# A feed-forward product in another seven-product form, and one batch's projection chunks moved together

## The chip, the cores and the metric

The kernel runs on one core of one Trainium2 chip. The metric is the device time of one execution, in microseconds; a comparison uses the median of several runs. One more execution was taken by the hardware profiler, and all durations of single instructions come from that one.

## The reference

For each of 8 batches there are a sequence `x` (8 heads x 512 x 64) and a state (8 heads x 32 x 64). Both attend to each other, and the result goes through a feed-forward layer with an exact GELU:

```python
scores = scale * x @ state^T            # softmax over the 32 states
xread  = softmax(scores) @ state        # 512 rows per batch
sread  = softmax(scale * state @ x^T) @ x   # 32 rows per batch
t   = concat([xread, sread], axis=2)    # (8, 8, 544, 64), heads merged to 512 columns
out = gelu(t.reshape(4352, 512) @ w_in) @ w_out   # w_in 512 x 2048, w_out 2048 x 512
```

Input and output are float32; the kernel multiplies in bfloat16 and accumulates in float32.

## The kernel before

**First product.** The 512 read rows of a batch are never formed. As `xread = a @ state`, the kernel multiplies the state by `w_in` first: `P` (256 rows of head and state x 2048) is made in four column chunks of 512 (`p_mm`, then copies to SBUF). A *block* `M(k)` is then 128 of the 2048 hidden columns for all 512 tokens of a batch: two matmuls of `P` with the transposed softmax weights `AT`, and a GELU on ACT, which writes `g` in bfloat16. A batch has 16 blocks; chunk f of `P` serves blocks 4f to 4f+3.

**Second product.** `g` (tokens x 2048) times `w_out` is done plainly for batch 0. For batches 1 to 7 both are cut in quarters: `g_q(b, h, k)` has token half h and hidden half k, `w_q[k][n]` has hidden half k and column half n. Seven products of quarters (`X(b, name)`, 16 matmuls of 128x256 each) stand in for eight. Some products need a sum or a difference of two quarters of `g` (`g_sum`, a DVE step over 128x2048, into one of three buffers of the pool `apool`) and of `w_out` (`w_sums`, once for all batches). The results are combined by ACT copies, DVE adds and, in the loop, two POOL steps per batch: `u` (line 658) and `v` (line 622). Four PSUM banks, tags `o0` to `o3`, hold the products; two products can be added up in one bank.

**Slots.** The loop over b = 2..7 is a *slot* each, with eight units p = 0..7. A unit issues two blocks of batch b, and most units one product X of batch b-1. Unit 1 also has the scores of batch b+1 (16 matmuls, exp on ACT), units 2 and 3 its normalisation (`norm`, three DVE steps), unit 5 the four chunks of the next `P` (`p_all`) and the first X of batch b, unit 7 the second X of batch b. In the last slot (b = 7) the 256 rows of state reads go through their own first product (`SR`, seven products in two halves g) in units 0 to 4, and through the second one (`R`) after that. The tail behind the loop does batch 7's remaining products; its last two are cut in three pieces (`PIECES`), so that the last copy and transfer are small.

**Order.** All is scheduled by hand: each engine runs its instructions in the order in which the program issues them, and waits in place for what it needs. SP holds the queue of output transfers (`x_out`, `rows_out`, `r_out`) and of the DMA transposes of `x` and of the softmax weights. POOL loads `x` and rearranges it (`rearr`, `rearr_ones`); a one-column copy (`hold_for`) keeps a load back until a given block of `g` is there.

Of the kernel before, what the change touches and what calls it, by code (L numbers as in the profile page):

```python
# [17 lines left out]
def kernel(  # L18
# [541 lines left out]
    w_sum = {}  # L560

    def w_add(name, x, y, op):
        if name == "3":
            pair = persist.tile([128, 2, MH, NH], BF16, name="ws_34", tag="mix0")
            w_sum["3"], w_sum["4"] = pair[:, 0], pair[:, 1]
        elif name != "4":
            tag = {"6": "mix1", "1": "mix2", "7": "mix3"}[name]
            w_sum[name] = persist.tile([128, MH, NH], BF16, name=f"ws_{name}", tag=tag)
        nc.vector.tensor_tensor(out=w_sum[name], in0=x, in1=y, op=op)

    def w_sums(i):
        (b11, b12), (b21, b22) = w_q
        w_add(*(
            ("3", b12, b22, ALU.subtract),
            ("4", b21, b11, ALU.subtract),
            ("6", b11, b12, ALU.add),
            ("1", b11, b22, ALU.add),
            ("7", b21, b22, ALU.add),
        )[i])
# [14 lines left out]
    def g_sum(b, name):  # L594
        (h0, k0), (h1, k1), op = G_SUMS[name]
        t = apool.tile([128, MH, 256], BF16, name="gsum", tag="gsum")
        nc.vector.tensor_tensor(out=t, in0=g_q(b, h0, k0), in1=g_q(b, h1, k1), op=op)  # L597
        xs[b, "g" + name] = t
# [20 lines left out]
    def c22(b):  # L619
        xs[b, "v"] = c_tile("v")  # L620
        o = xs[b, "o", 1]
        nc.gpsimd.tensor_tensor(  # L622
            out=xs[b, "v"], in0=xs[b, "q"], in1=o[:, :, :NH], op=ALU.subtract
        )
        if b < B - 2:
            c22_add(b)

    def c22_add(b):
        o = xs[b, "o", 1]
        nc.vector.tensor_tensor(out=o[:, :, NH:], in0=xs[b, 3], in1=xs[b, "v"], op=ALU.add)  # L630
        x_out(b, 1)

    def X(b, name):
        bank = {"3": 0, "4": 1, "5": 0, "2": 1, "1": 2, "6": 3, "7": 2}[name]
        first = name in "3416"
        if first:
            xs[b, bank] = otile([128, 2, NH], "xp", bank)
        ps = xs[b, bank]
        lhs = {"3": (0, 0), "4": (1, 1)}.get(name)
        lhs = xs[b, "g" + name] if lhs is None else g_q(b, *lhs)  # L640
        rhs = {"5": w_q[1][1], "2": w_q[0][0]}.get(name)
        rhs = w_sum[name] if rhs is None else rhs
        x_mm(ps, lhs, rhs, first)
        if name == "3":
            xs[b, "s3"] = c_tile("s3")
            if b > 1:
                nc.scalar.copy(out=xs[b, "s3"], in_=ps)
            for h in range(2):
                xs[b, "o", h] = hpool.tile([128, 2, d_model], FP32, name="oh", tag=f"oh{h}")
        elif name == "4":  # L650
            xs[b, "s34"] = c_tile("s34")
            nc.vector.tensor_tensor(out=xs[b, "s34"], in0=ps, in1=xs[b, "s3"], op=ALU.add)
        elif name == "5":
            o = xs[b, "o", 0][:, :, NH:]
            nc.scalar.copy(out=o, in_=ps)  # L655
            xs[b, "u"] = c_tile("u")
            x_out(b, 0, right)
            nc.gpsimd.tensor_tensor(out=xs[b, "u"], in0=xs[b, "s34"], in1=o, op=ALU.subtract)  # L658
        elif name == "2":
            nc.scalar.copy(out=xs[b, "o", 1][:, :, :NH], in_=ps)  # L660
            c22(b)
        elif name == "1":
            xs[b, "q"] = c_tile("q")
            nc.vector.tensor_tensor(out=xs[b, "q"], in0=ps, in1=xs[b, "s34"], op=ALU.add)
        elif name == "7":
            nc.vector.tensor_tensor(
                out=xs[b, "o", 0][:, :, :NH], in0=ps, in1=xs[b, "u"], op=ALU.add
            )
            x_out(b, 0, left)
# [8 lines left out]
    both = slice(0, 2)  # L678

    def L4():  # L680
        b = B - 1
        ps = xs[b, 1] = otile([128, 2, NH], "xp", 1)
        x_mm(ps, g_q(b, 1, 1), w_sum["4"], True)
        xs[b, "s34"] = c_tile("s34")
        nc.vector.tensor_tensor(out=xs[b, "s34"], in0=ps, in1=xs[b, "s3"], op=ALU.add)
        xs[b, "y"] = c_tile("q")
        nc.vector.tensor_tensor(out=xs[b, "y"], in0=xs[b, 3], in1=xs[b, "s34"], op=ALU.add)

    def L5():
        b = B - 1  # L690
        x_mm(xs[b, 0], xs[b, "g5"], w_q[1][1], False)
        nc.scalar.copy(out=xs[b, "o", 0][:, :, right], in_=xs[b, 0])
        rows_out(0, both, right, nc.sync)

    def L5_u():
        b = B - 1
        xs[b, "u"] = c_tile("u")
        nc.vector.tensor_tensor(
            out=xs[b, "u"], in0=xs[b, "s34"], in1=xs[b, "o", 0][:, :, right], op=ALU.subtract
        )  # L700

    def L2():
        b = B - 1
        x_mm(xs[b, 1], xs[b, "g2"], w_q[0][0], False)
        c21 = xs[b, "o", 1][:, :, left]
        nc.scalar.copy(out=c21, in_=xs[b, 1])
        rows_out(1, both, left, nc.sync)
        xs[b, "v"] = c_tile("v")
        nc.vector.tensor_tensor(out=xs[b, "v"], in0=xs[b, "y"], in1=c21, op=ALU.subtract)

    PIECES = ((0, 0, NH, 2), (1, 0, NH // 2, 0), (1, NH // 2, NH, 1))

    def l_mm(ps, name, j, n0, n1, first):
        for m in range(MH):
            nc.tensor.matmul(  # L715
                ps,
                lhsT=xs[B - 1, "g" + name][:, m, 128 * j:128 * j + 128],
                rhs=w_sum[name][:, m, n0:n1],
                start=(first and m == 0),
                stop=(m == MH - 1),  # L720
                skip_group_check=True,
            )

    def L1():
        b = B - 1
        for j, n0, n1, at in PIECES:
            ps = xs[b, "x", j, n0] = otile([128, n1 - n0], "xp", at)
            l_mm(ps, "1", j, n0, n1, True)
            nc.vector.tensor_tensor(
                out=xs[b, "o", 1][:, j, NH + n0:NH + n1],  # L730
                in0=ps,
                in1=xs[b, "v"][:, j, n0:n1],
                op=ALU.add,
            )
        rows_out(1, both, right, nc.sync)

    def L7():
        b = B - 1
        for j, n0, n1, at in PIECES:
            ps = xs[b, "x", j, n0]  # L740
            l_mm(ps, "7", j, n0, n1, False)
            nc.vector.tensor_tensor(
                out=xs[b, "o", 0][:, j, n0:n1], in0=ps, in1=xs[b, "u"][:, j, n0:n1], op=ALU.add
            )
            rows_out(0, slice(j, j + 1), slice(n0, n1), nc.scalar if n0 else nc.sync)
# [97 lines left out]
    def r_homes():  # L843
        pair = [att.tile([128, 2, MH, 128], BF16, name="rs", tag="xT") for _ in range(2)]
        one = att.tile([128, MH, 128], BF16, name="rs1", tag="AT")
        homes = [pair[0][:, 0], pair[0][:, 1], pair[1][:, 0], pair[1][:, 1], one]
        rs["homes"] = dict(zip("51267", homes))

    def r_sum(name):
        t = rs["g" + name] = rs["homes"][name]  # L850
        (h0, k0), (h1, k1), op = G_SUMS[name]
        nc.vector.tensor_tensor(out=t, in0=r_q(h0, k0), in1=r_q(h1, k1), op=op)
# [7 lines left out]
    def R(name):  # L860
# [4 lines left out]
        bank = {"3": 0, "4": 1, "5": 0, "2": 1, "1": 2, "6": 3, "7": 2}[name]  # L865
        first = name in "3416"
        if first:
            home = {"3": 1, "4": 2, "6": 2}
            rs[bank] = otile([128, NH], "rp", home[name]) if name in home else ftile([128, NH], "rp")
        ps = rs[bank]  # L870
        lhs = {"3": (0, 0), "4": (1, 1)}.get(name)
        lhs = rs["g" + name] if lhs is None else r_q(*lhs)
        rhs = {"5": w_q[1][1], "2": w_q[0][0]}.get(name)
        rhs = w_sum[name] if rhs is None else rhs
# [9 lines left out]
        add, sub = ALU.add, ALU.subtract  # L884
        if name == "3":
            nc.scalar.copy(out=c_new("s3"), in_=ps)
            for h in range(2):
                rs["o", h] = opool.tile([128, d_model], FP32, name="osb", tag="osb")
        elif name == "4":
            nc.vector.tensor_tensor(out=c_new("s34"), in0=ps, in1=rs["s3"], op=add)  # L890
        elif name == "5":
            o = rs["o", 0][:, NH:]
            nc.scalar.copy(out=o, in_=ps)
            nc.vector.tensor_tensor(out=c_new("u"), in0=rs["s34"], in1=o, op=sub)
        elif name == "1":
# [10 lines left out]
        elif name == "7":  # L906
            nc.vector.tensor_tensor(out=rs["o", 0][:, :NH], in0=ps, in1=rs["u"], op=add)
            r_out(0)
# [379 lines left out]
```

## Time and profile before

| | |
|---|---|
| median of 3 runs | 203.3 us (203.26, 203.30, 203.94) |
| profiled execution | 203.97 us, of which the profile's span is 202.1 us |
| granted TensorE clock | 1.00 |
| PE, matmul | busy 195.0 us (97% of the span) |
| DVE / ACT / POOL | busy 155.9 / 139.2 / 67.3 us |
| one product X | 16 matmuls, 1.75 us on PE |
| two blocks | 4 matmuls, 0.86 us on PE |
| one sum of `g` | mean 1.37 us on DVE, 35 of them |
| slot 3 to slot 4 | unit 0 begins at 72.31 and at 93.52 us |
| slot 4 to slot 5 | unit 0 begins at 93.52 and at 115.33 us |

All times of single instructions are counted from the start of the span. A line of a timeline gives start, duration, engine, line of the program, operation, what is written from what, shapes and a count; in brackets the idle time before it and the instruction that ended it. A line with a count over 1 is a run of instructions whose duration is that of the whole run.

### The profile page before, as it was taken

To read this page: it belongs to the slowest core of one execution; us is meant where nothing else is said; L and a number is where in the kernel's file an instruction comes from. 1 tells how busy PE (TensorE), PEld (TensorE's weight loads), DVE (VectorE), ACT (ScalarE), POOL (GpSimd) and SP (SyncE) were. 2 spreads that over 40 slices of the span, in tenths; PEclk is the share of its full clock that TensorE was granted. 3 is DMA by queue.
4 is the path that set the end of the run, shared out by engine and by line. 5 is a ranking of instruction groups with operands and counts; after the bars stand their busy time and mean duration, and the time that the engine had idled before them with its cause. 6 is when DMAs were issued, how large, how long until landed. Compare 5 with 4: busy or idle time off the path is not lost.

```text
span 202.1 us, 4900 instructions
## 1 busy us (share of the span) xinstructions
PE 195.0 (97%) x2030; PEld 134.4 (66%) x2035; DVE 155.9 (77%) x248; ACT 139.2 (69%) x251; POOL 67.3 (33%) x75
## 2 busy tenths in 40 slices
PE   7899999999999999999999999999999999999992
PEld 2434544465767677667767587677776878878892
DVE  2954875989996799986996967587758888894982
ACT  3785578798986878677967596688859477854020
POOL 8963503424259198431537202410220011200000
PEclk9999999999999999999999999999999999999999
DMA  6999999969665789592875208450107001040135
GB/s 195 196 171 203 205 199 194 181 140 158 89 116 107 208 96 156 116 133 78 107 156 148 63 2 112 146 114 0 52 27 184 3 0 55 0 159 0 52 105 159
DMA packets 40566, 23.16 MB, mean 115 GB/s; under 512 B 21856, under 2 KB 39136, under 8 KB 40544
## 3 DMA queue, kind: packets, MB, share of 16 engines
q0 software_dynamic: 13984, 8.10, 29.4%
q1 hardware_dynamic: 25872, 14.36, 29.3%
q10 hardware_dynamic: 688, 0.39, 0.6%
q8 instruction: 16, 0.26, 0.5%
q14 instruction: 6, 0.05, 0.1%
HBM read 17.30 MB, written 8.91 MB: 130 GB/s over the span
## 4 chain that ended last, share of the span: by engine, by line
PE 91%; DVE 5%; ACT 2%; issue 1%; ACTq 0%
PE xp L603 40%; PE hp L506 26%; PE op L548 5%; PE sp L810 3%; PE rp L876 3%; PE p_ps L441 2%; PE op L532 2%; PE xp L715 2%; PE pt L333 2%; PE warm_ps L150 2%; PE sr L917 1%; ACT P L955 1%; DVE gsum L597 1%; DVE P L955 1%; PE hp L1064 1%
## 5 line engine op out<-in xcount | busy, mean ns | idle before, releaser
L513 ACT ACTIVATE g<-hp 128x512 bf16<-128x512 f32 x124 | 65.9, 607 | 21.1 <-PE hp L506 14.8
L506 PE MATMUL hp<-AT,P 128*128 128x512 bf16 x248 | 61.2, 379 | 0.0
L603 PEld LDWEIGHTS <-gsum 128*128 128x128 bf16 x528 | 51.2, 98 | 11.4 <-DVE gsum L597 0.8
L597 DVE TENSOR_TENSOR gsum<-g 128x2048 bf16<-128x2048 bf16 x35 | 47.3, 1367 | 0.5
L506 PEld LDWEIGHTS <-P 128*128 128x128 bf16 x248 | 23.5, 98 | 20.6 <-issue 0.6
L603 PE MATMUL xp<-ws,gsum 128*128 128x256 bf16 x304 | 36.3, 273 | 0.4 <-DVE gsum L597 0.4
L603 PE MATMUL xp<-ws,g 128*128 128x256 bf16 x224 | 26.7, 272 | 0.3
L603 PE MATMUL xp<-w_out_bf,gsum 128*128 128x256 bf16 x224 | 26.6, 273 | 0.0
L603 PEld LDWEIGHTS <-g 128*128 128x128 bf16 x224 | 21.7, 98 | 5.3 <-issue 1.9
L658 POOL TENSOR_TENSOR u<-s,oh 128x512 f32<-128x512 f32 x6 | 8.8, 1468 | 40.1 <-ACT oh L655 40.1
L225 POOL COPY x<-xb 128x1024 bf16<-128x1024 bf16 x12 | 14.6, 1244 | 17.5 <-DMA xb<-in_x_dram 17.5
L622 POOL TENSOR_TENSOR v<-q,oh 128x512 f32<-128x512 f32 x6 | 8.3, 1379 | 19.5 <-ACT oh L660 17.2
L235 POOL COPY xo<-xb 128x1024 bf16<-128x1024 bf16 x12 | 12.1, 1041 | 5.0 <-PE sr L917 5.0
L955 ACT CAST P<-p_ps 128x512 bf16<-128x512 f32 x25 | 12.7, 606 | 0.1
L356 DVE TENSOR_TENSOR a<-e,ics 128x512 bf16<-128x512 bf16 x14 | 11.7, 834 | 0.5
L548 PE MATMUL op<-w_out_bf,g 128*128 128x512 bf16 x44 | 11.1, 380 | 0.5 <-issue 0.3
L955 DVE CAST P<-p_ps 128x512 bf16<-128x512 f32 x15 | 9.4, 684 | 1.7 <-PE p_ps L441 1.7
L353 DVE TENSOR_REDUCE cs<-e 128x16 f32<-128x512 bf16 x14 | 9.5, 677 | 0.9 <-ACT e L340 0.9
L441 PE MATMUL p_ps<-w_in_bf,sbd 64*32 64x512 bf16 x248 | 9.4, 380 | 0.0
L513 ACT ACT_TABLE_LOAD x7 | 9.0, 1283 | 0.1
L548 PEld LDWEIGHTS <-g 128*128 128x128 bf16 x48 | 4.2, 98 | 5.6 <-issue 0.8
L340 ACT ACT_TABLE_LOAD x6 | 7.7, 1283 | 0.1
(143 smaller groups left out, 240.7 us busy)
## 6 DMA issues: line engine op xcount, KB each, us to landing
out_dram<-oh SPq DMA_DIRECT2D x15, 256.0 KB, 2.5
xb<-in_x_dram POOLq DMA_DIRECT2D x7, 512.0 KB, 5.9
out_dram<-oh SPq DMA_DIRECT2D x6, 512.0 KB, 3.5
w_in_bf<-in_moe_w_in_dram POOLq DMA_DIRECT2D x6, 256.0 KB, 12.2
out_dram<-osb SPq DMA_DIRECT2D x5, 256.0 KB, 3.2
w_out_bf<-in_moe_w_out_dram POOLq DMA_DIRECT2D x4, 256.0 KB, 8.6
w_out_bf<-in_moe_w_out_dram POOLq DMA_DIRECT2D x2, 512.0 KB, 13.5
x0f<-in_x_dram SPq DMA_DIRECT2D x3, 256.0 KB, 3.9
```

Source lines behind the costliest of these rows:

```text
L225: nc.gpsimd.tensor_copy(out=A.x4[:, :, :, 64 * t:64 * t + 64].rearrange("p j c d -> p c j d"), in_=src[:, t],)
L235: eng.tensor_copy(out=A.xo[:, :, :, 2 + 64 * t:66 + 64 * t].rearrange("p j c d -> p c j d"), in_=src[:, t],)
L353: nc.vector.reduce_sum(out=cs, in_=e4, axis=AX.X)
L356: nc.vector.tensor_tensor(out=A.a[:, :, hs].rearrange("p g (c n) -> p g c n", n=NS), in0=e4, in1=ics[:, :, :].to_broadcast((128, G, 2, NS) ...
L441: nc.tensor.matmul(ps[t][32 * c:32 * c + 32, :], lhsT=sbd[64 * t:64 * t + 64, b, c, 32 * t:32 * t + 32], rhs=w_in_bf[64 * t:64 * t + 64, c ...
L506: nc.tensor.matmul(hp, lhsT=Ps[b][:, t, m * 128:(m + 1) * 128], rhs=atts[b].AT[:, :, t, :], start=(t == 0), stop=(t == 1),)
L513: nc.scalar.activation(out=gs[b][:, m, :], in_=hp, func=AF.Gelu)
L548: nc.tensor.matmul(ops[b, j], lhsT=gs[b][:, m, j * 128:(j + 1) * 128], rhs=w_out_bf[:, m, :], start=(m == 0), stop=(m == MC - 1),)
L597: nc.vector.tensor_tensor(out=t, in0=g_q(b, h0, k0), in1=g_q(b, h1, k1), op=op)
L603: nc.tensor.matmul(ps[:, j - js[0], :], lhsT=lhs[:, m, 128 * j:128 * j + 128], rhs=rhs[:, m, :], start=(first and j == js[0] and m == 0), ...
L658: nc.gpsimd.tensor_tensor(out=xs[b, "u"], in0=xs[b, "s34"], in1=o, op=ALU.subtract)
L955: copy(out=Ps[b][:, t, f * 512:(f + 1) * 512], in_=ps[t])
```

## The change

The product becomes another form of seven products. Which quarter stands in which place is fixed by `chain` and `w_diff`; in `chain`, a11 = `q(0,1)`, a12 = `q(0,0)`, a21 = `q(1,1)`, a22 = `q(1,0)`. Three products (1, 2, 4) take a quarter of `g` as it is. The other four take sums that build on one another: 5 = a21 + a22, 6 = 5 - a11, 7 = a11 - a21, 3 = a12 - 6; likewise four of `w_out`. Products 1, 6 and 7 are added up in one bank and read between: after 1 by a DVE add, after 6 by an ACT copy (`u`), after 7 by two DVE adds; 5 and 3 share another bank. Each of 2, 4, 6 and 5 is copied to SBUF by ACT (`snap`); POOL takes no part. Per batch there are four sums of `g` where there were five, four DVE adds as before, four ACT copies where there were three. In a slot the products stand in the order 1, 6, 5, 7 in units 0 to 3, then 3, 2 in unit 5 and 4 in unit 7, where there were 4, 5, 1, 2, then 7, 3 and 6. The matmuls are the same in number and shape.

In slot 2, chunks 2 and 3 of batch 2's `P` were made in units 0 and 3, each behind the unit's blocks. Now both stand in one run behind unit 2's product, and unit 2 issues blocks 4 to 7 while unit 3 issues none.

In the tail, product 5 and the last one, 3, are cut in pieces; product 7 stands whole before 3, with its two adds and one output transfer of 512 KB, where two transfers of 256 KB went out earlier.

```diff
+    def w_diff(name):
...
+        x, y = {
+            "5": (b12, b11),
+            "6": (b22, w_t.get("5")),
+            "7": (b22, b12),
+            "4": (b21, w_t.get("6")),
+        }[name]
+        nc.vector.tensor_tensor(out=w_t[name], in0=x, in1=y, op=ALU.subtract)
...
+    def chain(name, q, got):
+        a11, a12, a21, a22 = q(0, 1), q(0, 0), q(1, 1), q(1, 0)
+        return {
+            "1": (a11,),
+            "2": (a12,),
+            "4": (a22,),
+            "5": (a21, a22, ALU.add),
+            "6": (got.get("5"), a11, ALU.subtract),
+            "7": (a11, a21, ALU.subtract),
+            "3": (a12, got.get("6"), ALU.subtract),
+        }[name]
...
+    BANK = {"2": 0, "1": 1, "6": 1, "7": 1, "5": 2, "3": 2, "4": 3}
...
     def X(b, name):
...
+        x_mm(ps, x_lhs(b, name), w_rhs(name), first)
+        if name == "2":
             if b > 1:
+                snap(b, "c2", "c2", ps)
+        elif name == "4":
+            snap(b, "c4", "c4", ps)
+        elif name == "1":
             for h in range(2):
                 xs[b, "o", h] = hpool.tile([128, 2, d_model], FP32, name="oh", tag=f"oh{h}")
+            add(xs[b, "o", 0][:, :, left], ps, xs[b, "c2"])
+            x_out(b, 0, left)
+        elif name == "6":
+            snap(b, "u", "u", ps)
         elif name == "5":
+            snap(b, "s5", "s5", ps)
+        elif name == "7":
+            add(xs[b, "o", 1][:, :, right], ps, xs[b, "s5"])
+            add(xs[b, "o", 1][:, :, left], ps, xs[b, "c4"])
+            x_out(b, 1)
+        elif name == "3":
+            add(xs[b, "o", 0][:, :, right], ps, xs[b, "u"])
             x_out(b, 0, right)
...
-            M(k, k + 1)
-            if b == 2 and p == 0:
-                pmat(2, 2)
-            if b == 2 and p == 3:
-                p_copy_s(2, 3, p_mm(2, 3, ftile))
+            if b != 2 or p != 3:
+                M(k, k + 1)
+            if b == 2 and p == 2:
+                M(k + 2, k + 3)
             if b == 2 and p == 1:
-                w_sums(4)
-            if p < 4 or (p == 4 and nb == B):
+                w_diff("7")
+            if p < 5 and nb < B:
                 if p == 0:
-                    g_sum(b - 1, "5")
-                    if b > 2:
-                        sr_w("5216"[b - 3])
-                X(b - 1, "45127"[p])
-                if p < 3:
-                    g_sum(b - 1, "127"[p])
+                    g_sum(b - 1, "56")
+                if p == 2:
+                    g_sum(b - 1, "7")
+                if p == 3:
+                    g_sum(b - 1, "3")
+                if p < 4:
+                    X(b - 1, "1657"[p])
+                if b == 2 and p == 2:
+                    for x in [(2, f, p_mm(2, f, ftile)) for f in (2, 3)]:
+                        p_copy(*x)
+                if p == 1 and b > 2:
+                    sr_w("5216"[b - 3])
...
     b = B - 1
-    for name in "521":
-        g_sum(b, name)
-    L4()
-    g_sum(b, "7")
+    g_sum(b, "56")
+    X(b, "1")
+    g_sum(b, "73")
     L5()
-    L5_u()
-    L2()
-    R("7")
-    L1()
-    L7()
+    X(b, "6")
+    R("3")
+    X(b, "7")
+    L3()
```

The state reads' second product `R` takes the same form; its sums are `r_sum("56")` in unit 4 and `r_sum("73")` in unit 5 of the last slot, its products 2, 4 stand in unit 5, 1, 6, 5 in unit 6, 7 in unit 7 and 3 in the tail. The first product of the state reads (`SR`) keeps its form; in unit 0 of the last slot `sr_w("7")` moves from before to behind the products.

## The prediction

> **What bounds the kernel now.** I read the page's shares first, then the chain that ended last, then each engine's timeline around the eight units of a slot. The page's first part and the head of the chain:
>
> ```profile
> PE 195.0 (97%) x2030; PEld 134.4 (66%) x2035; DVE 155.9 (77%) x248; ACT 139.2 (69%) x251; POOL 67.3 (33%) x75
> ...
> PE 91%; DVE 5%; ACT 2%; issue 1%; ACTq 0%
> ```
>
> PE is the bound. In PE's timeline it stands still after 13.2 us only in pieces of tenths; the rest of DVE's 5% lies in the first 13 us, which the change leaves alone. The piece that this change can touch is in slot 4 (PE's timeline; in brackets the wait and its releaser):
>
> ```profile
> 112.93 0.22 PE L424 MATMUL srT<-ident,srm 128*128 128x128 bf16 x1
> 113.57 1.92 PE L603 MATMUL xp<-ws,gsum 128*128 128x256 bf16 x16 [0.42 <-DVE gsum L597]
> ```
>
> From srT to the next product 0.64 us pass here; in slot 3 it is 0.05 (91.72 to 91.77). The stall is worth 0.59.
>
> After X's last matmul, the end is DVE's last piece, its transfer (198.88 + 2.3 to landing = 201.2) and 0.9 us more. So the time is PE's own work plus waits on PE, plus that end. What decides is whether DVE's order feeds PE in time. DVE and POOL in slot 3 and the slot's first product on PE:
>
> ```profile
> 71.62 3.16 DVE L597 TENSOR_TENSOR gsum<-g 128x2048 bf16<-128x2048 bf16 x1
> ...
> 71.67 2.03 POOL L235 COPY xo<-xb 128x1024 bf16<-128x1024 bf16 x2
> ...
> 73.71 1.12 POOL L967 COPY hold<-g 128x1 bf16<-128x1 bf16 x1
> ...
> 75.91 0.68 DVE L652 TENSOR_TENSOR s<-xp,s 128x512 f32<-128x512 f32 x1
> ...
> 76.65 1.96 POOL L225 COPY x<-xb 128x1024 bf16<-128x1024 bf16 x1 [1.01 <-DMA xb<-in_x_dram]
> ```
>
> A sum of 1.22 us takes 3.16 while POOL copies: they do not run together, and POOL, 0.05 later, went first.
>
> **Part by part.** PE's matmuls are the same in number, shape and place, so PE's own work is unchanged but for one item. Durations: a product of 16 matmuls 1.75, a pair of blocks 0.86, a sum 1.22, a DVE add from PSUM 0.69 (a next one starts 0.61 later), norm 1.61 to the next start.
>
> *Removed, hidden already.* One of five g sums per batch (7 x 1.22 on DVE), one of five weight sums (1.25), twelve POOL steps u and v (17.1 us). None is on the chain except the sum at the end of a slot: X6 in unit 7 needed g6, X4 in its place reads g itself. That removes slot 4's stall: **-0.59**.
>
> *P chunks together.* One chunk alone costs PE 0.34 + 0.10 on the next group (51.17 to 51.51, then 1.85 in place of 1.75), two alone 0.88; a run of two at 36.92 costs 0.56 + 0.11 = 0.67. **-0.21**. Blocks 4 to 7 need four PSUM tiles, whose gelus follow on ACT behind the exps (54.4), a table load (1.28), two gelus (1.08) and the u copy (0.59), four at 0.5: they end at about 57.8 to 59.3. The run starts at 59.3: just covered, up to 0.2 if not.
>
> *ACT.* Four copies a batch for three (0.59 more). The c4 copy falls into the 1.4 us idle ahead of the gelus at 137.22, the s5 copy into 0.9 ahead of 145.47: nothing. Without that cover each would be 0.6 a slot.
>
> *New wait in every slot.* X1, X6 and X7 share one bank, so X6 waits until DVE's add has read X1. In slot 6: X1 ends at 139.15, the add runs 139.35 to 140.04, X6 is due at 140.48: 0.44 spare, as scores and a pair of blocks lie between. The chained sums 5 and 6 end by 138.34 there: nothing. SP issues as many transfers as before; the softmax transpose behind `x_out(1)` goes out by 149.3 here (150.85 now) and at 65.5 in slot 2, as now: nothing.
>
> *Slot 3.* Sum 5 ends at 74.78 as now; sum 6 waits for it (74.81 to 76.03); the add starts at 75.95 and ends at 76.64; X6 is due at 76.25 and starts near 76.69: 0.44, or 0.63 if the hold copy (0.19) slips between. Behind it on DVE are two sr_w sums (1.28), norm and sum 7: if POOL's two copies from 76.65 take their 2.0 us first, sum 7 ends at 82.7, when X7 is due at 81.9: 0.8 more. Between 0 (both sums clear POOL) and 1.4 I take **+0.50**, nearest to the row. As to the chain's link: a dependent DVE step starts 0.03 after the end of its source (62.16 after 62.12), an independent one 0.08 before it, so a link costs 0.11. The Trainium skill (VectorE: DVE Perf Modes, The DRAIN you can't avoid) has it that a wait between two such steps costs nothing extra; by that the 0.50 would be 0.39.
>
> *Slot 2.* The order from 50.15: pair, X1, scores (0.47), pair, X6, four blocks, X5 (57.57), the P run (59.32), X7 (59.99), four blocks, X3 at 63.47. DVE's two P copies now stand ahead of norm and sum 3. The first starts 0.51 after the run (51.61 after 51.10), so 59.76; the second 0.60 later; norm 60.96; sum 3 from 62.57 to 63.79; X3 starts at 63.83: **+0.36**. Before, the g sum there had 2 us to spare. The other end: the hold copy at 51.56 meets sum 6, which starts at 51.49. If the sum goes first, hold, the load of x and both POOL copies behind it come 1.1 later, and norm meets them at 62: 1.45. I take the small end, since in slot 3 a sum that was 0.05 ahead lost.
> The Trainium skill (SBUF — State Buffer, Who interferes with whom) says that of such a pair whichever starts first holds the port for its whole instruction. By that rule hold would lose here and the term would be 1.45; the slot 3 row speaks against it at so small a lead.
>
> *Slot 7.* The two adds behind X7 now stand on DVE ahead of the add that reads SR1's bank, into which SR7 accumulates:
>
> ```profile
> 172.96 0.69 DVE L827 TENSOR_TENSOR srt<-srt 128x512 f32<-128x512 f32 x1
> ...
> 174.08 1.49 DVE L831 TENSOR_TENSOR srt<-sp,srt 128x512 f32<-128x512 f32 x2 [0.44 <-PE sp L810]
> ...
> 175.19 0.61 PE L810 MATMUL sp<-srx,srw 128*128 128x128 bf16 x8
> ```
>
> Adds at 173.65 and 174.26, SR1's at 174.87 to 175.56 where it ended at 174.77; SR7 was due at 175.19: **+0.41** (0 to 0.5). The gelus behind it reach R2 with 0.5 spare.
>
> *The end.* X7 starts at 194.82 (its wait for ACT's u copy, 194.78, just fits), its two adds end at 198.07 and only then one transfer of 512 KB leaves, where 256 KB left at 197.11; L3's three pieces follow in the same queue. The last DVE piece stays near 198.9, and the transfers are the end now:
>
> ```profile
> out_dram<-oh SPq DMA_DIRECT2D x15, 256.0 KB, 2.5
> ...
> out_dram<-oh SPq DMA_DIRECT2D x6, 512.0 KB, 3.5
> ```
>
> 198.11 + 3.5 = 201.6 against 201.2 now: 0.4. If the 256 KB of pieces queue wholly behind it at 350 GB/s (the window from 199 to 200 us) it is 0.75 more: 1.15. If mid-kernel traffic swells the 3.5, nothing. I take **+0.60**.
>
> Sum: -0.59 - 0.21 + 0.50 + 0.36 + 0.41 + 0.60 = +1.07. The profiled execution took 203.97 (span 202.1 and 1.9 around it), so 205.0 for its like. The runs' median of 203.3 lies 0.67 below it: 204.4.
>
> **Rivals.** *Not slower:* the freed DVE and POOL do feed PE in time. With u and v gone POOL's copies move, and if slot 3's sum 6 ends before 75.5 and slot 2's sum 3 before 63.4, both chain waits (0.86) vanish: 203.5; below 202.3, where faster by over 0.5% begins, it comes only if slot 7 and the end go too and PE's small gaps at 0.16 close. For it: DVE loses 1.22 us a slot; against it: both spots are set by what DVE waits for, not by its load.
> *POOL first:* slot 2 at 1.45 and slot 3 at 1.3: +1.09 + 0.8, 206.3. For it: leads of 0.05 to 0.1 us decide; against: the row of slot 3.
> *The last transfer hidden:* without the end's 0.60, 203.8. For it: at 200 to 201 us the engines move only 22 GB/s; against: 256 KB more leave 1 us later.
> That X6's wait for the add costs in every slot (the edit does not then do its work) is part of the forecast's wide end only: 0.44 spare was read in a slot where DVE is idle 1.07 before it.
>
> **How the numbers follow.** 0.5%, or 1.02 us, is about what a measurement of this kernel can tell from no change. Forecast 0.47 (204.4 +- 0.5, on the edge: 0.30 slower, 0.17 same); not slower 0.24 (0.18 same, 0.06 faster); POOL first 0.21, slower; transfer hidden 0.08, same. So faster 0.06, same 0.43, slower 0.51. All costs at their small ends give 203.3 - 0.80 = 202.5, all at their large ends (1.4, 1.45, 0.5, 1.15) 207.0; leaving out 1 in 10 on each side, 202.8 to 206.0. The likeliest case's own range is 203.9 to 204.9.
>
> **What would show it.** In the profile after: no PE wait ahead of unit 7's product in slot 4; a PE wait on DVE's add of some 0.4 to 0.6 at X6 in slot 3; one of 0.4 on sum 3 at X3 in slot 2; one of 0.4 at SR7 in the last slot; and 2.2 us or more from the last matmul's end to the last landing, with a 512 KB transfer issued near the last DVE step. It is wrong if X6 waits in slots 4 to 6, if PE waits on ACT, or if the slot length of an undisturbed slot (21.21 us from 72.31 to 93.52) changes.

## The result, and the profile after

The changed kernel takes 206.7 us (median of 6 runs, 206.49 to 207.42), the kernel before 203.62 in the runs beside it: a ratio of 1.0155, interval 1.0127 to 1.0182. It is slower by 3.1 us. The profiled execution took 207.1 us with a span of 205.2, against 203.97 and 202.1, also 3.1 more.

From the page after, the engines' busy times:

```profile
PE 195.5 (95%) x2035; PEld 134.1 (65%) x2035; DVE 142.9 (70%) x234; ACT 142.8 (70%) x260; POOL 50.6 (25%) x63
```

DVE is busy for 13 us less, 11.7 of it in the sums of `g` and `w_out`, and POOL for 17 us less, as the removed combining steps promise. PE's own work is the same within 0.5 us. Yet PE's share falls from 97% to 95%: engines with less to do feed PE later. PE's waits say where. The first is at the start, for a load (line waited in, tile and line waited for; total, times, longest):

```profile
PE xT_ps L271 <- DMA xb<-in_x_dram: 0.7, 1, 0.7
```

The others stand in PE's timeline, whose rows answer to those shown of before:

```profile
65.93 1.92 PE L623 MATMUL xp<-w_out_bf,gsum 128*128 128x256 bf16 x16 [1.73 <-DVE gsum L613]
...
78.93 1.91 PE L623 MATMUL xp<-ws,gsum 128*128 128x256 bf16 x16 [0.25 <-DVE oh L642]
...
115.61 0.22 PE L424 MATMUL srT<-ident,srm 128*128 128x128 bf16 x1
115.67 1.91 PE L623 MATMUL xp<-ws,g 128*128 128x256 bf16 x16
...
177.66 0.61 PE L781 MATMUL sp<-srx,srw 128*128 128x128 bf16 x8 [0.22 <-DVE srt L802]
```

First X3 in slot 2, then X6 in slot 3, then slot 4's end, where the stall is gone (0.06 from srT to the next product, 0.64 before), last SR7. How these add up, from the first product of each slot in the two profiles:

| stretch | before | after | difference |
|---|---|---|---|
| start to the transposes of the second x block (L271) | 19.21 | 19.81 | +0.60 |
| from there to unit 0 of slot 3 | 53.10 | 54.77 | +1.67 |
| slot 3 | 21.21 | 21.62 | +0.41 |
| slot 4 | 21.81 | 21.22 | -0.59 |
| unit 0 of slot 5 to the last matmul's end | 83.19 | 83.56 | +0.37 |
| behind the last matmul | 3.58 | 4.22 | +0.64 |

These give +3.1. The last row is good to 0.05 only, since it rests on spans that are given to 0.1 us. The second row holds the P run (-0.21 by the prediction) and the stall at X3 (so 1.88). Its cause begins 14 us earlier. The timelines of DVE, POOL and SyncE's queue in slot 2, after:

```profile
52.09 1.23 DVE L613 TENSOR_TENSOR gsum<-gsum,g 128x2048 bf16<-128x2048 bf16 x1
...
52.16 1.21 POOL L927 COPY hold<-g 128x1 bf16<-128x1 bf16 x1 [1.41 <-ACT g L513]
...
53.30 0.88 POOL L117 DMA_DIRECT2D xb<-in_x_dram  x1
...
54.35 0.39 SPq L637 DMA_DIRECT2D out_dram<-oh  x1
...
60.35 2.02 POOL L225 COPY x<-xb 128x1024 bf16<-128x1024 bf16 x2 [6.17 <-DMA xb<-in_x_dram]
...
60.51 1.29 DVE L453 CAST P<-p_ps 128x512 bf16<-128x512 f32 x2 [2.31 <-PE p_ps L441]
...
62.31 2.49 POOL L235 COPY xo<-xb 128x1024 bf16<-128x1024 bf16 x2
...
62.71 1.19 DVE L356 TENSOR_TENSOR a<-e,ics 128x512 bf16<-128x512 bf16 x1
...
63.82 2.05 DVE L613 TENSOR_TENSOR gsum<-g,gsum 128x2048 bf16<-128x2048 bf16 x1
```

And POOL and SyncE's queue of before at the same place:

```profile
51.56 0.19 POOL L967 COPY hold<-g 128x1 bf16<-128x1 bf16 x1 [1.41 <-ACT g L513]
...
52.08 0.88 POOL L117 DMA_DIRECT2D xb<-in_x_dram  x1 [0.33 <-POOL hold L967]
...
57.70 0.39 SPq L617 DMA_DIRECT2D out_dram<-oh  x1
...
57.97 2.48 POOL L225 COPY x<-xb 128x1024 bf16<-128x1024 bf16 x2 [5.02 <-DMA xb<-in_x_dram]
```

Sum 6 starts 0.07 us ahead of the hold copy. A copy of one column that took 0.19 now takes 1.21: it ends 0.05 behind the end of the sum. The load that it keeps back goes out at 53.30 in place of 52.08, POOL has its block at 60.35 in place of 57.97, and so POOL's copies run from 60.35 to 64.80, just where DVE has norm's multiplication (1.19 in place of 0.69) and sum 3 (2.05 in place of 1.22). Sum 3 ends at 65.87, X3 starts at 65.93.

Slot 2 itself begins at 50.15 before and at 50.74 after, so 0.6 of each of these differences belongs to the start of the kernel. Counted from the slot's beginning, the load goes out 0.6 later and its block is in use 1.8 later. The other 1.2 is the load itself, 7.05 us from issue to use in place of 5.89. The new form also sends 256 KB of product 1's rows at 54.35, 1.05 behind this load; before, the transfer there left at 57.70, 5.6 behind it. No run moves that transfer alone, so how much of the lateness is the copy's and how much the transfer's is not shown; the P run alone, below, says something on it.

At the end of the kernel, the queue of SyncE after:

```profile
200.62 0.35 SPq L637 DMA_DIRECT2D out_dram<-oh  x1
...
201.09 1.13 SPq L680 DMA_DIRECT2D out_dram<-oh  x2
```

The 512 KB leave at 200.62, 0.36 before the last matmul ends (200.98). The last bytes land at 203.63, 2.65 behind the last matmul; before it was 200.73, 2.2 behind (2.0 and 1.7 behind in the profiles of before once more and of the P run alone, which have the same tail).

### The profile page after: what moved, and what is told of

Same layout as the page of the kernel before. It is cut to its first block, busy times and chain, and to the rows that moved or that the text cites. A ratio compares the mean times of both kernels' runs of the same rounds, so it can differ in the third digit from the quotient of the medians.

```text
span 205.2 us, 4865 instructions
## 1 busy us (share of the span) xinstructions
PE 195.5 (95%) x2035; PEld 134.1 (65%) x2035; DVE 142.9 (70%) x234; ACT 142.8 (70%) x260; POOL 50.6 (25%) x63
## 4 chain that ended last, share of the span: by engine, by line
PE 79%; DMA 8%; POOL 4%; DVE 3%; ACT 2%; issue 1%; DVEq 0%; ACTq 0%; POOLq 0%
PE xp L623 39%; PE hp L506 23%; DMA xb<-in_x_dram 8%; PE op L548 4%; PE rp L847 3%; PE sp L781 3%; POOL w_in_bf L105 2%; PE op L532 2%; DVE oh L642 2%; PE p_ps L441 1%; ACT P L915 1%; PE pt L333 1%; PE sr L877 1%; DVE gsum L613 1%; PE xp L694 1%
## 5 line engine op out<-in xcount | busy, mean ns | idle before, releaser
L623 PEld LDWEIGHTS <-gsum 128*128 128x128 bf16 x416 | 40.4, 98 | 11.7 <-DVE gsum L613 2.2
L623 PEld LDWEIGHTS <-g 128*128 128x128 bf16 x336 | 32.5, 98 | 6.9 <-issue 1.6
L623 PE MATMUL xp<-w_out_bf,g 128*128 128x256 bf16 x224 | 26.7, 273 | 0.3
L613 DVE TENSOR_TENSOR gsum<-g 128x2048 bf16<-128x2048 bf16 x14 | 19.0, 1356 | 0.5
L646 ACT COPY c<-xp 128x512 f32<-128x512 f32 x14 | 8.3, 593 | 9.8 <-PE xp L623 4.5
L623 PE MATMUL xp<-ws,g 128*128 128x256 bf16 x112 | 13.4, 273 | 0.0
L623 PE MATMUL xp<-w_out_bf,gsum 128*128 128x256 bf16 x96 | 11.5, 273 | 1.7 <-DVE gsum L613 1.7
L642 DVE TENSOR_TENSOR oh<-xp,c 128x512 f32<-128x512 f32 x14 | 9.6, 686 | 4.3 <-PE xp L623 4.3
L642 DVE TENSOR_TENSOR oh<-xp,u 128x512 f32<-128x512 f32 (+2 forms) x9 | 5.0, 569 | 9.9 <-PE xp L623 9.9
L613 DVE TENSOR_TENSOR gsum<-g,gsum 128x2048 bf16<-128x2048 bf16 x7 | 9.4, 1339 | 0.0
```

The lines of the kernel that those rows point to most:

```text
L613: nc.vector.tensor_tensor(out=got[name], in0=x, in1=y, op=op)
L623: nc.tensor.matmul(ps[:, j - js[0], :], lhsT=lhs[:, m, 128 * j:128 * j + 128], rhs=rhs[:, m, :], start=(first and j == js[0] and m == 0), ...
L642: nc.vector.tensor_tensor(out=out, in0=x, in1=y, op=ALU.add)
L646: nc.scalar.copy(out=xs[b, name], in_=ps)
```

## The experiments

Below, *body* is the time from the first transpose of L271 to the end of the last matmul: it leaves out the load at the start and the tail, and so shows PE's waits in the slots alone. All but the medians are from profiled executions; the column behind the last matmul is again good to 0.05.

| kernel | body | behind the last matmul | median of runs |
|---|---|---|---|
| before | 179.31 | 3.58 | 203.6 |
| changed | 181.17 | 4.22 | 206.7 |
| hold copy early | 179.85 | 4.18 | 205.31 |
| P copies on ScalarE | 179.28 | 4.24 | 204.64 |
| form alone | 180.32 | 4.17 | 205.63 |
| P run alone | 179.51 | 3.19 | 203.93 |
| adds of X7 late | 180.84 | 4.15 | 206.06 |
| output in halves | 181.22 | 3.81 | 206.16 |
| X5 ahead of X6 in slot 3 | 181.66 | 4.25 | 206.33 |
| four edits | 178.48 | 3.86 | 203.32 |
| four edits, one issue on ScalarE | 178.48 | 3.91 | 203.41 |
| the same, hold copy early | 178.48 | 3.91 | 204.07 |

The runs of before beside these had a median of 203.62 for the changed kernel, 203.81 for the next four, 203.54 for the four after them (adds late to four edits) and 203.42 for the last two.

**The hold copy early.** Theory: the small copy's lost race starts the stall in slot 2.

```diff
-                hold_for(b, 0)
+                hold_for(*((1, 15) if b == 2 else (b, 0)))
```

> In slot 2 the copy that holds back the load of x waits for block 15 of batch 1 instead of block 0 of batch 2, so it runs before sums 5 and 6 start. Theory A (the port): sum 6 took the port 0.07 us ahead of the hold copy, which ended 1.1 us late; the load and POOL's four copies behind it came late and met norm and sum 3. Then PE's wait on sum 3 at X3 falls from 1.73 us to 0.4 or less and the time by 1.3 to 1.9, to about 205.0. Theory B (DVE's order): the two P copies ahead of norm and sum 3 make X3 late whatever POOL does; then the wait stays over 1.2 and the time at 206.7.

Measured 205.31 us, ratio to before 1.0075 (1.0051 to 1.0099). DVE, POOL and PE in slot 2:

```profile
50.07 0.19 POOL L927 COPY hold<-g 128x1 bf16<-128x1 bf16 x1
...
56.95 2.49 POOL L225 COPY x<-xb 128x1024 bf16<-128x1024 bf16 x2 [5.65 <-DMA xb<-in_x_dram]
...
62.68 1.22 DVE L613 TENSOR_TENSOR gsum<-g,gsum 128x2048 bf16<-128x2048 bf16 x1
...
63.96 1.92 PE L623 MATMUL xp<-w_out_bf,gsum 128*128 128x256 bf16 x16 [0.39 <-DVE gsum L613]
```

The copy starts 0.13 ahead of sum 5 (50.20) and takes its 0.19, POOL is out of the way by 61.4, sum 3 takes its 1.22, and X3's wait falls from 1.73 to 0.39. The body is 1.32 shorter. So POOL's late copies made 1.3 of the 1.9 us. The edit does more than remove the race: the load goes out 1.6 us earlier in its slot than it did before the change, and 3.3 ahead of product 1's transfer. The rest is DVE's order: the two P copies ahead of norm and sum 3.

**The P copies on ScalarE.** All four copies of the run on ACT (two of them were on DVE), nothing else.

```diff
-                        p_copy(*x)
+                        p_copy_s(*x)
```

> Both P copies of the run in slot 2 go to ACT, so DVE has none of them ahead of norm and sum 3; the hold stays as it is. Theory B (DVE's order): X3's wait vanishes, the time falls by 1.7 to 1.9, to 204.9. Theory A (the port alone): POOL's late copies still meet norm or sum 3 and hold one of them by 1 to 2 us; X3's wait stays at 0.5 to 1.5. If the wait vanishes here and in the run with the early hold, it takes both: the copies ahead on DVE and POOL's late copies.

Measured 204.64 us, ratio 1.0043 (1.0026 to 1.006). The wait at X3 is gone altogether, though the hold copy is blocked as before:

```profile
51.63 1.21 POOL L927 COPY hold<-g 128x1 bf16<-128x1 bf16 x1 [1.40 <-ACT g L513]
...
59.58 1.22 DVE L613 TENSOR_TENSOR gsum<-g,gsum 128x2048 bf16<-128x2048 bf16 x1 [0.30 <-PE xp L623]
...
59.80 2.89 POOL L225 COPY x<-xb 128x1024 bf16<-128x1024 bf16 x2 [6.14 <-DMA xb<-in_x_dram]
```

Without the P copies, DVE is through with norm and starts sum 3 at 59.58, before POOL's late copies; this time the sum goes first, and POOL waits (2.89). So 0.6 of the 1.9 us is the P copies' alone, and 1.3 need both: the P copies push norm and sum 3 back past 60, and the late load puts POOL's copies there. Each edit alone takes most of it away, which is why the two gains (1.3 and 1.9) don't add. The body is 179.28; the other terms, slots 3 and 7 as measured, put it at 179.31 - 0.59 - 0.21 + 0.41 + 0.38 = 179.30.

**The form alone.** P chunks 2 and 3 back in units 0 and 3, blocks in their units.

```diff
-            if b != 2 or p != 3:
-                M(k, k + 1)
-            if b == 2 and p == 2:
-                M(k + 2, k + 3)
+            M(k, k + 1)
+            if b == 2 and p == 0:
+                pmat(2, 2)
+            if b == 2 and p == 3:
+                p_copy_s(2, 3, p_mm(2, 3, ftile))
...
-                if b == 2 and p == 2:
-                    for x in [(2, f, p_mm(2, f, ftile)) for f in (2, 3)]:
-                        p_copy(*x)
```

> The new form of the product alone; chunks 2 and 3 of batch 2's P stand in units 0 and 3 of slot 2 as in the kernel before, and no block is ahead. My theory: DVE's P copy in unit 0 stands ahead of sums 5 and 6, so sum 6 ends at 54.7 and the add at 55.4 on the clock of before, while X6 is due at 54.5: a PE wait of 0.9 at X6 in slot 2, no wait of 1.7 at X3, and 0.21 for the chunks apart; 0.8 below the changed kernel, 205.9. Rival (the form alone is harmless and the moved chunks do the damage): no wait in slot 2, 205.0 or less.

Measured 205.63 us, ratio 1.0085 (1.0057 to 1.0113). The theory was right in kind: a wait at X6 and none at X3. The timeline of slot 2:

```profile
51.86 0.19 POOL L927 COPY hold<-g 128x1 bf16<-128x1 bf16 x1 [1.40 <-ACT g L513]
...
51.91 0.69 DVE L453 CAST P<-p_ps 128x512 bf16<-128x512 f32 x1 [1.40 <-PE p_ps L441]
...
52.52 1.22 DVE L613 TENSOR_TENSOR gsum<-g 128x2048 bf16<-128x2048 bf16 x1
...
55.65 1.91 PE L623 MATMUL xp<-ws,gsum 128*128 128x256 bf16 x16 [0.65 <-DVE oh L642]
```

Here a P copy still stands ahead of the sums in unit 0, so the first sum starts at 52.52 and the hold copy goes through in 0.19. But the chained sums are then late, and X6 waits 0.65 in slot 2. The change as a whole removed this wait by moving the copy away, and by the same move brought sum 6 onto the hold copy. With the copy in time, POOL has the block at 58.25, 7.8 behind the beginning of the slot, as before.

**The P run alone**, on the kernel before: the block lines of the diff above in the other direction, with the old form kept.

> The kernel before with only the P chunks moved: both in one run behind unit 2's product of slot 2, blocks 4 to 7 ahead. My theory: PE saves 0.21, the two DVE copies stand ahead of norm alone, as this form has no sum in unit 3: 0.2 faster, the same within what can be measured, with slot 2 at 0.2 less. Rival (the moved chunks do the damage by themselves, through the hold copy and POOL): 1 to 2 us slower.

Measured 203.93 us, ratio 1.001 (0.999 to 1.003). Neither the 0.21 nor a loss shows in the runs. In the profile slot 2 takes 22.36 in place of 22.16: a block waits on a P copy of DVE, and what is lost there is more than the 0.21. POOL, and the block's wait on PE:

```profile
52.16 1.08 POOL L967 COPY hold<-g 128x1 bf16<-128x1 bf16 x1 [1.40 <-ACT g L513]
...
53.18 0.88 POOL L117 DMA_DIRECT2D xb<-in_x_dram  x1
...
58.96 2.25 POOL L225 COPY x<-xb 128x1024 bf16<-128x1024 bf16 x2 [4.90 <-DMA xb<-in_x_dram]
...
62.94 1.68 PE L506 MATMUL hp<-AT,P 128*128 128x512 bf16 x7 [0.25 <-DVE P L453]
```

The hold copy loses its race here too, behind a sum of the old form. Yet the block is in use 5.78 behind the load's issue, 0.4 later in its slot than before and not 1.8, and the old form sends its 256 KB only at 57.81. So the lost race by itself did not make the long delay there, and the P copies on DVE and the lost race together, without the new form, cost 0.2. The run brings its gain only where the copies behind it are in time, as in the four edits together below.

**The adds of X7 behind the state adds**, in slot 7: the third argument makes X leave out its adds and its transfer, which `x7_adds` then issues.

```diff
-            X(c, "7")
+            X(c, "7", True)
             SR("1", 1)
             SR("6", 1)
+            x7_adds(c)
```

> In slot 7 product 7's two adds and its output transfer are issued behind the adds of the second half's state products 1 and 6, no longer ahead of them; all else as in the changed kernel. Theory (state product 7 waits because its operand's add stands behind product 7's two adds in VectorE's queue, worth 0.39 us): the 0.22 us wait of the state product on the state add is gone, the time is 0.4 us below the changed kernel's 206.7, some 206.3. Rival (VectorE simply has too much in this stretch, and the two adds come due again at once): a wait of 0.2 to 0.4 us shows up on a later product of slot 7 or on product 3, and the time stays at 206.7.

Measured 206.06 us, ratio 1.0113 (1.008 to 1.0146). No wait is left in slot 7, none came in its place, and the slot is 0.38 shorter (the body 0.33, as slot 2's wait is 1.77 here): the term is as the prediction had it.

**The last 512 KB in two halves.**

```diff
             add(xs[b, "o", 1][:, :, right], ps, xs[b, "s5"])
+            if b == B - 1:
+                x_out(b, 1, right)
             add(xs[b, "o", 1][:, :, left], ps, xs[b, "c4"])
-            x_out(b, 1)
+            x_out(b, 1, left if b == B - 1 else slice(None))
```

> In the last stretch alone, the 512 KB transfer of product 7's rows is sent as two of 256 KB, the right half of the columns after the first add and the left half after the second; all else as in the changed kernel. Theory (the end is later by 0.65 us because 512 KB is issued in one piece behind two adds of about 0.7 us each): the first half starts some 0.7 us earlier and the end comes 0.2 to 0.5 us earlier, 206.2 to 206.5 against 206.7. Rival (the end is set by the small pieces of product 3 and their fixed time from issue to landing, whatever stands ahead of them): the last transfer ends at the same distance from the last matmul as before, 4.2 us, and the time stays at 206.7.

Measured 206.16 us, ratio 1.0124 (1.0088 to 1.016). The body is unchanged (181.22), the tail some 0.4 shorter:

```profile
199.34 0.97 SPq L637 DMA_DIRECT2D out_dram<-oh  x2
```

The first half leaves 0.95 before the last matmul ends (200.29), and from 200.3 to 201.8 the queue moves 83 to 95 KB in each quarter of a microsecond without a break. It looks as if the end waits for the bytes of the last rows; no run changed their number, so that is not shown.

**X5 ahead of X6 in slot 3.**

```diff
-                    X(b - 1, "1657"[p])
+                    X(b - 1, ("1567" if b == 3 else "1657")[p])
```

> In slot 3 alone, product 5 is taken in unit 1 and product 6 in unit 2, so that product 6 no longer stands one unit behind the add that still reads its bank; all else as in the changed kernel. Theory (product 6 loses 0.42 us in slot 3 to the add of product 1, which comes late because sum 6 shares VectorE's port with the hold copy and the block copies): the wait is gone and the time is 0.4 us below 206.7, some 206.3. Rival (slot 3 loses the same time at the next product, because VectorE's queue as a whole is late): a wait of 0.3 us or more on product 6 or 7 in units 2 and 3, and 206.7.

The rival was right. X6's wait is gone, and one on sum 7 comes two units later:

```profile
82.63 1.22 DVE L613 TENSOR_TENSOR gsum<-g 128x2048 bf16<-128x2048 bf16 x1
...
83.91 1.92 PE L623 MATMUL xp<-ws,gsum 128*128 128x256 bf16 x16 [0.59 <-DVE gsum L613]
```

DVE's queue as a whole is late in slot 3. The body is 0.49 longer, 0.36 of it in slot 3. The median, 206.33 (ratio 1.0132, 1.0097 to 1.0167), is all the same not above the changed kernel's. In the profiles the start was 0.72 shorter here (L271 at 19.09); that this holds for the medians too is not shown.

**Four edits together**: the P copies on ScalarE and the three above.

> Four edits on the changed kernel together: the four copies of the P chunks of slot 2 on ScalarE, product 5 ahead of product 6 in slot 3, product 7's adds in slot 7 behind the state adds, and the last 512 KB in two transfers. If the costs found so far are separate and add up: the run with the copies alone gave 204.64; less 0.42, 0.39 and 0.2 to 0.5 this is 203.3 to 203.6, at or a little under the kernel before (203.8 over 20 runs), since the stall of slot 4 that the change removes (0.59) and the P run (0.21) are then not given back. If the waits only move (VectorE is the limit in these stretches): 204.2 to 204.7.

Measured 203.32 us against 203.54 for before, ratio 0.9984 (0.9959 to 1.0009): no difference that these runs can tell. The profile has no wait of PE in slots 2 to 7 that is longer than 0.15, and the body is 178.48, 0.83 under that of before; the prediction's two gains, 0.59 and 0.21, make 0.80. They lie where it put them: slot 4 takes 21.21 in place of 21.81, and slot 2 21.93 in place of 22.16, a length that before has in both its profiles. The swap in slot 3, useless alone, pays once the P copies are off DVE: of the 0.80 between this body and the one with the copies alone, 0.38 is slot 7's term, and the other 0.42 the wait of X6. Of the 0.83 the tail takes back 0.3.

**One issue on ScalarE**, and then the hold copy early on top of it. The second half of the 512 KB goes out through ScalarE's queue; the second kernel adds the first experiment's edit.

```diff
-        x_out(b, 1, left if b == B - 1 else slice(None))
+        if b == B - 1:
+            x_out(b, 1, left, nc.scalar)
+        else:
+            x_out(b, 1)
```

> The four edits together, and in the last stretch the second 256 KB transfer of product 7's rows is issued by ScalarE instead of SyncE. Theory (the end hangs on the last issue of SyncE, which is back to back with four issues and ends 1.08 us after the last matmul with the four edits, 0.5 us before the change): SyncE then has three issues, the last ends some 0.7 us after the last matmul, the span ends 3.5 to 3.6 us after it, not 3.86, and the time is 203.0 against 203.3. Rival (the bytes or the landing time of the last transfers bind): 3.86 us and 203.3.

> As the run before, and in slot 2 the copy that releases the load of block 4 reads the last g tile of batch 1, so that it is free a unit earlier. Theory (with the P copies on ScalarE there is no wait left on sum 3 in slot 2): no difference to the run before, 203.0. Rival (the load of block 4 and the block copies on GpSimd still cost other steps of slots 2 and 3): 0.2 to 0.4 us lower.

The first is 203.41 against 203.42 (ratio 1.0014, 0.9994 to 1.0034); its queues at the end:

```profile
197.14 0.40 ACTq L637 DMA_DIRECT2D out_dram<-oh  x1
197.46 0.85 SPq L690 DMA_DIRECT2D out_dram<-oh  x2
```

SyncE's last issue ends 0.82 behind the last matmul in place of 1.08, and the span still ends 3.91 behind it. The theory that the end hangs on SyncE's issues falls; the last bytes landed 2.2 behind the last matmul in both kernels of this experiment and in the four edits. The second took 204.07 (ratio 1.0022, 1.0007 to 1.0037) with the same body to the hundredth, so the early load is worth nothing once X3 does not wait; its higher median is not in the profile.

**Both kernels once more**, unchanged.

> The kernel before, unchanged, profiled a second time. If the stall of slot 4 (0.42 us on sum 7's operand, of 0.59 that the prediction took off) belongs to every execution, it is there again at product 7 of slot 4; if it comes from one late step of that one execution, it is gone and the span is under 202.1. The lead (first transpose of the second x block at 19.2 us) may move by up to 0.8 us.

> The changed kernel, unchanged, profiled a second time. If the 0.7 us wait on the x load at 19.8 us is no part of the change, the transposes start at 19.0 to 19.3 us and the span is some 204.5; the waits of 1.7 to 1.9 us on sum 3 in slot 2, of 0.25 on the add in slot 3 and of 0.22 in slot 7 are there again.

204.05 and 207.28 us in one run each. The stall of slot 4 is there again in before, to the hundredth:

```profile
113.77 1.92 PE L603 MATMUL xp<-ws,gsum 128*128 128x256 bf16 x16 [0.42 <-DVE gsum L597]
```

In the changed kernel the hold copy again loses to sum 6 by 0.07 (52.11 and 52.18, 1.21 long), and the three waits are 1.91, 0.25 and 0.22. The transposes of L271 start at 19.83 there, which was not expected; they start at 19.01 to 19.51 in the nine kernels that differ from it only in later slots, and at 19.81 in the P run alone. The nine have the same code as it up to there. So the 0.6 at the start is not made by that code. What PE waits for there is loads: 0.73 for one of x in the first profile of the changed kernel, 0.44 for one of weights and 0.14 for x in the second. What decides it is open. The body repeats to 0.17 in the changed kernel, nearly all of it the wait at X3, and to 0.47 in before, 0.35 of it ahead of slot 2, where one wait for a weight load (0.28) differs.

## Why the prediction was wrong

The direction and the places were right: X3 in slot 2, X6 in slot 3, nothing in slots 4 to 6, SR7 in slot 7, a later end, and the stall of slot 4 gone. The likeliest of its three outcomes came in. The time lies outside its range, at 206.7 against 204.4 and an upper end of 206.0. From profile to profile it forecast +1.07 where +3.1 was measured; of the 2.1 between them slot 2 is 1.5 and the start 0.6, and the other terms are right within 0.1.

- *Slot 2* is the step that failed: +0.36 was forecast and 1.88 measured. The working had both ends, 0.36 and 1.45, and described the long chain as it came (hold, load, POOL's copies, norm). It chose the small end because in slot 3 a sum that started 0.05 ahead had lost to POOL. In slot 2 the sum was 0.06 to 0.07 ahead and won, in both profiles of the changed kernel and in the six others in which the two meet there. Both ends were also some 0.2 to 0.4 short: without POOL's late copies X3 still waits (body 179.85 against 179.28, so 0.57), and with them the block was in use 1.8 later in its slot, not 1.1, so that sum 3 itself, not only norm, met POOL. The working counted SyncE's transfers, found as many as before and put them at nothing; that one of 256 KB now leaves 1.05 behind this load, where it left 5.6 behind, it did not look at. In the P run alone, without that transfer, the lost race made the block 0.4 later.
- *The page of the Trainium skill that spoke against that choice* (SBUF — State Buffer, Who interferes with whom: a DVE step with two SBUF inputs and a GpSimd step that reads SBUF contend for a shared port, and whichever issues first has it for its whole instruction) was the better guide in slot 2. In slot 3 the recorded starts still go against it, after as before: the sum takes 3.13 though POOL's copy starts 0.01 later.

```profile
73.89 3.13 DVE L613 TENSOR_TENSOR gsum<-g 128x2048 bf16<-128x2048 bf16 x1
...
73.90 2.03 POOL L235 COPY xo<-xb 128x1024 bf16<-128x1024 bf16 x2
```

So a lead of 0.01 to 0.05 in the records does not tell who comes first, and one of 0.07 did here. In the form alone a sum and a POOL copy both start at 58.25, and there the sum takes its 1.22 and the copy waits. With 1.45 in the sum the forecast would have been 205.5, 0.6% under the measured time. The rival called POOL first (206.3) is the nearest in time, in part by luck: it had slot 2 still too small (1.45 for 1.88) and slot 3 too large (1.3 for 0.41). It had a chance of 0.21; with half of that above 206.3, the prediction's own chances put more than one time in ten above its upper end of 206.0.
- *The start* (+0.60 in the profile) was in no term. It moved between 19.01 and 19.83 in the fourteen profiles, with waits for loads.
- *Slot 3*: 0.50 forecast, 0.41 measured. *Slot 7*: 0.41 and 0.38. *The end*: 0.60 forecast, some 0.65 in these two profiles; before's own tail was 3.19 to 3.58 in three executions of its form, so 0.6 to 1.0.
- *Slot 4*: -0.59 and -0.59. *The P run*: -0.21, outweighed where its copies are late (P run alone: slot 2 0.20 longer), and there in slot 2 of the four edits (-0.23).
- *A dependent step on DVE*: after too, sum 6 starts 0.03 behind the end of sum 5 (50.83 and 1.23 long), and the add behind sum 3 starts 0.07 before that sum ends (65.80, 65.87). That link, which the Trainium skill (VectorE: DVE Perf Modes, The DRAIN you can't avoid) puts at nothing for a row of copies, is 0.10 here, too little to decide anything in this case.
- *From profiled to median*: 0.67 was taken off; after, the profiled execution lay 0.4 above the median. Before's two profiled executions lie 0.4 above its median of 203.6, the four edits' one does not. That is why 0.6 less in the span is only 0.2 less by the medians; what makes before's median run quicker than its profiled ones stays open.

## What to carry to other kernels

Work taken off an engine moves everything behind it earlier, and the first thing to look for is which small step of another engine it now meets: here a gate of 0.2 us in front of a load became one of 1.2, and the load then ran beside another transfer. Where steps of two engines hold each other up and start within a tenth of a microsecond, don't rest on the cheap end (here the sum lost such a race in slot 3 and won one in slot 2), or remove the race by giving the small step data that is ready earlier. And before moving copies into a stretch, list what stands behind them in the queue of their engine: here the copies alone cost 0.6 us, the late load alone nothing, and both together 1.9.

## What the runs showed of the hardware that was not expected

A GpSimd copy of one column, 0.19 us by itself, took 1.21 behind a VectorE sum with two SBUF inputs that started 0.07 earlier. A load of 512 KB was in use 7.05 us behind its issue where a transfer of 256 KB was issued 1.05 behind it, and 5.89 and 5.78 behind where that came 5.6 and 4.6 behind it (before, the P run alone). With the transfer 3.3 behind it was 5.88 once and 6.53 once (form alone, early hold), so that the one makes the other is not shown. At the end of the kernel, whether one engine or two issued the last transfers and whether the last issue came 0.3 earlier made no difference: the last bytes landed 2.2 us behind the last matmul in both.
